# Block 0's last chunk by one level of Strassen's method, its second product beside the next block's first

## The chip, the core and the metric

The kernel runs on one core of one Trainium2 chip. The metric is the device time of one execution in microseconds (us); the time of a kernel is the median of its runs. Six parties matter here: TensorE (PE in the profile), which multiplies; VectorE (DVE), ScalarE (ACT) and GpSimd (POOL), which work elementwise; SyncE (SP), whose queue issues most transfers; and the DMA engines, which move data between HBM and the on-chip memory.

## The reference, cut to what matters

```python
kv  = np.einsum('bhsd,bhse->bhde', k, v)        # 8 batches, 8 heads, 576 rows, head size 64
out = np.einsum('bhsd,bhde->bhse', q, kv)
x   = out / sqrt(mean(out**2, -1) + 1e-6) * g_norm
x   = x.transpose(0, 2, 1, 3).reshape(4608, 512)  # rows x d_model
h   = x @ w_in                                  # w_in 512 x 2048
g   = np.maximum(0.01 * h, h)
return g @ w_out                                # w_out 2048 x 512
```

`w_in` and `w_out` arrive as float64. The kernel reads them as pairs of 32-bit words and rounds them to float32 on the chip.

## The kernel before, in words

**Tiling.** The 4608 rows of x are cut into 9 blocks of 512 rows (`NB`), and d_ff = 2048 into 4 chunks of 512 columns (`NC`; a chunk is 2 halves of 2 slices of 128, `U = 2`). For each block and chunk there are two products, both 512 x 512 x 512: h = W1 chunk times x block, and o = g chunk times W2 chunk, where o is summed over the chunks. x of a block is made by the attention part (`attention`, `outputs`, `divide`), whose steps are put between matmuls of the block before.

**How a chunk is multiplied.** Block 0 multiplies plainly (`first_block`, L1335). I call 2048 streamed columns a *unit*: for h, one slice of 128 d_ff columns, which is 4 matmuls of 128x512; for o, the same slice against 4 row groups, as 4 matmuls of 128x512 or 8 of 128x256. A plain chunk is 4 units for h and 4 for o. From block 1 on a chunk is multiplied by Strassen's method (`strassen`, L865): 7 products of 256 x 256 x 256 blocks, each 4 matmuls of 128x256, in the order `1, 2, 6, 5, 7, 3, 4`. Products 1, 6, 7 and 4 add up in one PSUM bank, 2, 5 and 3 in another, and after most of them ACT copies the bank or DVE adds it to SBUF before the next product may go on in that bank. Block 1 uses one level (`product_h`, `product_o`); later blocks use two levels for part of the work. The trace counts each float32 matmul as two records, so "x8" is 4 matmuls.

**What Strassen needs beside the products.** Sums of weight quarters for h (`sides_w1`, 4 additions of 128x512 a chunk, on GpSimd) and for o (`sides_w2`, 4, on GpSimd), sums of x quarters (`sides_x`, 4, on DVE, once a block), and sums of g quarters (`sums_of`, 4 a chunk, GpSimd, tiles `gs1` to `gs4`). `combine` makes the weight sums of the second level while block 1 runs: 8 additions on GpSimd (parts 0 and 1) and 8 on DVE (part 2) a chunk. They go to HBM for the later blocks.

**Rounding the weights.** The 32 weight tiles (`w_jobs`, here *jobs*) are loaded as raw 512 KB pieces into a ring of 7 places, 4 of them in `pairs`, which later holds Strassen's weight sums. A job is rounded by `round_f64` (L253): two ACT operations (`add`, `cut`; L271, L269), then on DVE a clamp (L273), a shift (L278), an or (L280) and an integer add (L285; two for a *halved* job). The temporaries live in the same `gs` tiles.

**Order.** Matmuls, rounding and most of SP's loads are held in program order (`pin`). In block 0 `between` (L1383) puts rounding jobs and attention steps after each half unit. The additions of `add` (L709) and the ACT operations on h and x were not held in order there; the builder's scheduler places them. In block 1 the second product of a chunk runs one chunk behind the first: `o_queue` holds `product_o`, and after `LAG = 2` slots one o product is issued beside each h product.

```python
        while half and rounded < min(3 * n + 8, 2 * n + 13, len(w_jobs) - (n < 11)):
            ...
            round_w(rounded)
            rounded += 1
```

After block 0's last unit its four accumulators are copied to `o_all` (L1371, L1373) and written out; then block 1 begins with chunk 0's h alone, because no o product is queued yet.

Of the kernel before, what the change touches and what calls it, by code (L numbers as in the profile page):

```python
# [11 lines left out]
U32 = mybir.dt.uint32  # L12
I64 = mybir.dt.int64
# [11 lines left out]
def kernel(  # L25
# [68 lines left out]
    steady = first_done = in_line = False  # L94

    def in_turn(ins):

        if steady or in_line:
            pin(ins)

# [126 lines left out]
    def spare(n, name, dtype=F32):  # L227
# [3 lines left out]
    raw_homes = itertools.cycle([view(stage, i * NW, NW) for i in range(3)]  # L231
                                + [pair(i, NW) for i in range(4)])
# [15 lines left out]
    def load_f64(src, eng):  # L248
        raw = next(raw_homes).bitcast(U32)
        load(split(raw, src), src, eng)  # L250
        return raw.rearrange("p (n two) -> p n two", two=2)
# [44 lines left out]
    w_jobs[1:-1] = [w_jobs[i + 1 if i % 2 else i - 1] for i in range(1, len(w_jobs) - 1)]  # L296
# [3 lines left out]
    def load_w(j, *eng):  # L300
        eng = eng or (nc.sync,)
        dst, src = w_jobs[j]
        if w_in.dtype == I64:
            w_raws[j] = load_f64(src.bitcast(U32), eng)
# [8 lines left out]
    def round_w(j):  # L313
        for _ in rounding(j):
            pass

# [73 lines left out]
    def outputs(b, lo, hi, e, sums, kv=None):  # L390


        x, n = x_of(lo, hi), hi - lo
        tiles = att_tiles("o_ps")
        o_ps = [t[:, :n] for t in tiles]
        o_products(b, lo, hi, e, o_ps)
        if kv is not None:
            kv_beside(b + 1, kv, tiles)
        for l in range(2):
            sq = t2k(n, "sq" if e else f"sum{l}")  # L400
            nc.scalar.activation(sq, o_ps[l], func=AF.Square)
            if e == 0:
                sums.append(sq)
            else:
                in_turn(nc.vector.tensor_add(sums[l], sums[l], sq))
        for l in range(2):
            nc.scalar.activation(x[:, 2 * l + e, :], o_ps[l], func=AF.Copy, scale=g_sb[:, e:e + 1])

    def divide(lo, hi, sums):
# [3 lines left out]
        for l in range(2):  # L413
# [4 lines left out]
            if l:  # L418
                act = nc.scalar.activation(rms, rms, func=AF.Sqrt, scale=1.0 / D, bias=eps_sb)
                if first_done:  # L420
                    pin(act)
# [3 lines left out]
        for l in range(2):  # L425
            t = t2k(n, "spread")
            nc.scalar.copy(t.rearrange("p (a i) -> p a i", i=E),
                           rms[:, l, :].unsqueeze(2).to_broadcast([P, n // E, E]))
            spread.append(t)
# [11 lines left out]
    def both_outputs(b, lo, hi, sums, kv=None, banks=None):  # L441
# [9 lines left out]
        for l in range(2):  # L451
            sq = t2k(2 * n, "sq").rearrange("p (e n) -> p e n", e=2)
            nc.scalar.activation(sq, o_ps[l], func=AF.Square)
# [9 lines left out]
        for l in range(2):  # L463
            for e in range(2):
                nc.scalar.activation(x[:, 2 * l + e, :], o_ps[l][:, e, :], func=AF.Copy,
                                     scale=g_sb[:, e:e + 1])
# [24 lines left out]
    def tail_of(b, lo, hi, fine=False, kv=(None, None), banks=None):  # L491
# [15 lines left out]
        for _ in divide(lo, hi, sums):  # L507
            if fine:
                yield
# [7 lines left out]
    def attention(b, apart=True, fine=False):  # L517
# [17 lines left out]
        for m in range(2):  # L535
# [9 lines left out]
            if not apart and m == 0:  # L545
                for p in (2, 3):
                    load_pair(b, p)
# [154 lines left out]
    later, tick = [], 0  # L702
# [5 lines left out]
    def add(eng, out_, a, b_, minus=False, pinned=False):  # L708
        ins = eng.tensor_tensor(out_, a, b_, op=ALU.subtract if minus else ALU.add)  # L709
        if pinned or steady:  # L710
            pin(ins)

    def sides_w1(c):
# [4 lines left out]
        s12 = pair(0, U, 2, 2, P)  # L718
        sides = {1: a11, 2: a12, 4: a22, 5: s12[:, :, :, 0, :], 6: s12[:, :, :, 1, :]}
        add(nc.gpsimd, sides[5], a21, a22)  # L720
        add(nc.gpsimd, sides[6], sides[5], a11, True)

        def more():
            s34 = pair(1, U, 2, 2, P)
            sides.update({7: s34[:, :, :, 0, :], 3: s34[:, :, :, 1, :]})
            add(nc.gpsimd, sides[7], a11, a21, True)
            add(nc.gpsimd, sides[3], a12, sides[6], True)
# [5 lines left out]
    writes = []  # L733

    def sides_w2(n):
# [7 lines left out]
        def sums(i):  # L743
            t = (t12, t34)[i]
            if n >= NC:
# [8 lines left out]
            if n == NC - 1:  # L754

                writes.append((w2_dram[c][i], t))
            else:
                pin(nc.sync.dma_start(w2_dram[c][i], t))
# [15 lines left out]
    def combine(c, part):  # L774
# [4 lines left out]
        parts = [((5, 6), pair(0, U, 2, 2, P))], [((7, 3), pair(1, U, 2, 2, P))], \  # L779
# [122 lines left out]
    def relu(t, src=None):  # L902
        with tc.issue_after(behind.pop()) if behind else nullcontext():
            nc.scalar.activation(t, t if src is None else src, func=AF.Prelu, alpha=SLOPE)  # L904
# [32 lines left out]
    def product_h(c, w_sides, x_sides, to):  # L937
# [3 lines left out]
        def done(i, bank):  # L941

            if i == 1:
                nc.scalar.copy(g11, bank)
            elif i == 5:
                nc.scalar.copy(g22, bank)
# [3 lines left out]
            elif i == 6:  # L950
                nc.scalar.copy(g21, bank)
# [9 lines left out]
        yield from strassen((("ha", "hc"), ("hb", "hd"))[c % 2], lambda i, part, r: w_sides[i][:, part, r, :],  # L961
                            lambda i, part, r: x_sides[i][:, r, :], done)
        yield from sums_of(c, to)

    more = consts.tile([P, 19, P], F32, name="more")
# [366 lines left out]
    def first_block(between):  # L1335

        accs = [ps_m.tile([P, DM], F32, tag=t, name="o_acc") for t in ("oa", "oc", "hb", "hd")]
        x, last = xTs.pop(0), None
        for n in range(2 * NC * U + 1):
            now = last  # L1340
            if n < 2 * NC * U:
                c, h, u = n // (2 * U), n // U % 2, n % U
                h_ps = ps_m.tile([P, NT], F32, tag=("ha", "hc")[n % 2], name="h_ps")

                parts = 2 if n == 0 else 1
                for part in range(parts):
                    cols = slice(part * NT // parts, (part + 1) * NT // parts)
                    for e in range(NE):
                        matmul(h_ps[:, cols], lhsT=w1_sb[h][c][:, u, e, :],
                               rhs=x[:, e, cols], start=(e == 0 and part == 0),  # L1350
                               stop=(e == NE - 1), skip_group_check=True)
                gT = view(g_all[n // 4 % 2], n % 4 * NT, NT)
                act = nc.scalar.activation(gT, h_ps, func=AF.Prelu, alpha=SLOPE)
                if n == 2 * NC * U - 1:
                    pin(act)
                last = (gT, w2_rows(h, c, u), n)
            if now is None:
                continue
            between(n, 0)
            for t in range(4):  # L1360
                halves = now[2] // U % 2
                for v in range(1 + halves):
                    cols = slice(v * N2, v * N2 + N2) if halves else slice(0, NT)
                    matmul(accs[t][:, cols], lhsT=now[0][:, t * P:(t + 1) * P],
                           rhs=now[1][:, v, :],
                           start=(now[2] == 0), stop=(n == 2 * NC * U), skip_group_check=True)
            between(n, 1)
        for t in range(4):
            o = o_homes[t].rearrange("p u n -> p (u n)")
            if t % 2:  # L1370
                nc.scalar.copy(o, accs[t])  # L1371
            else:
                nc.vector.tensor_copy(o, accs[t])  # L1373
            nc.scalar.dma_start(out[t * P:(t + 1) * P, :], o)

    first_attention()
    steps = {i: tail for tail in [tail_of(0, NT, S)] for i in (6, 8, 10)}
    a_steps = attention(1, False)
    steps.update((i, a_steps)
                 for i in (12, 13, 15, 16, 19, 20, 22, 23, 24))  # L1380
    loaded, rounded = 7, 5

    def between(n, half):  # L1383
        nonlocal loaded, rounded
        go(steps.get(2 * n + half, iter(())), 1)

        while half and rounded < min(3 * n + 8, 2 * n + 13, len(w_jobs) - (n < 11)):
            if loaded < len(w_jobs):
                load_w(loaded)
                loaded += 1  # L1390
                if loaded in (15, 19):
                    load_pair(1, (loaded - 15) // 4)
            round_w(rounded)
            rounded += 1
        if (n, half) == (12, 0):
            for p in range(2):
                load_pair(2, p)

    first_block(between)
    first_done = True  # L1400
    x_sides, _, sums, _ = sides_x(1)
    for _ in sums:
        pass
    for i, r in ((1, 0), (0, 1)):
        nc.gpsimd.tensor_copy(pair(i, U, 2, 2, P)[:1, 0, 0, r, :1], w2_1[:1, 1, NC - 1, U - 1, :1])
    h_sides, more_h = sides_w1(0)
    more_h()
    for part in range(2):
        sides_w2(0)[1](part)
    for part in range(2):  # L1410
        combine(0, part)
# [8 lines left out]

    SLOTS_3 = 10, 20, 22, 23
    WRITES_3 = 20, 21, 22, 23, 24, 25

    LAG = 2

    SPREAD = (2, 3, 9, 10, 12)
    o_queue, waited = collections.deque(), 0
# [8 lines left out]

    def go_o():
        while o_queue:
            if next(o_queue[0], o_queue) is not o_queue:
                return True  # L1440
            o_queue.popleft()

    for i in range(1, NB):
# [6 lines left out]
        for c in range(NC):  # L1450
# [7 lines left out]
            for t in range(7):  # L1458
                slot = 7 * c + t
                tick += 1  # L1460
                while later and later[0][0] <= tick:
                    later.pop(0)[1]()
# [39 lines left out]
                if slot == 4 and not one:  # L1502
                    while writes:
                        pin(nc.sync.dma_start(*writes.pop()))
                if one:
# [84 lines left out]
```

## Time and profile before

| | |
|---|---|
| median of 3 runs | 908.23 us (908.08 to 908.59) |
| the profiled execution, its own time | 908.56 us |
| its span, first to last instruction | 906.6 us |
| granted TensorE clock | 1.00 throughout |
| PE, busy share of the span | 99% |
| DVE, ACT, POOL | 67%, 37%, 58% |
| first unit of block 0 starts | 22.29 us |
| block 1's first product starts | 138.65 us |
| block 2's first product starts | 225.41 us |

The profiled execution took 908.56 us by its own time, of which 906.6 us lie between its first and its last instruction, so 1.96 us lie around the span. Every duration in this document is one record or one group of records of a profiled execution. In the views, "start us, us" are the start of a group and its length; the arrow shows the output tile, then the inputs; a bracket at the end says how long the engine sat idle before it and what ended that.

### The profile page before, as it was taken

Reading aid. Unit: us, or ns where it says so; the run is one execution under the profiler, and the core shown is the slowest. Engines: PE = TensorE matmul, PEld = TensorE weight load, DVE = VectorE, ACT = ScalarE, POOL = GpSimd, SP = SyncE. Lnnn points to the kernel's source line nnn. Section 1 sums busy time; section 2 is a strip of 40 time slices with the busy share of each in tenths; the row PEclk is TensorE's granted clock in tenths of the full one; section 3 lists DMA queues with packets and bytes.
Section 4 is the critical chain, followed back from the end, with each engine's and each line's share of the span. In section 5 each row is a group of like instructions: output and inputs, shape, how many; then the busy total and the mean of one; then the engine's idle time right before and its main releaser. Section 6 shows DMA issues by size and latency. Waiting matters only on the chain.

```text
span 906.6 us, 19091 instructions
## 1 busy us (share of the span) xinstructions
PE 899.4 (99%) x7344; PEld 789.7 (87%) x7344; DVE 610.8 (67%) x942; ACT 331.2 (37%) x645; POOL 525.0 (58%) x672
## 2 busy tenths in 40 slices
PE   8999999999999999999999999999999999999998
PEld 5555558888998999999999999999999999999997
DVE  5996856576674767685977498666877584646453
ACT  5663413231234332434333433343243424232420
POOL 2000255976738765766757584758477847883730
PEclk9999999999999999999999999999999999999999
DMA  9888436977799688968897798958886778677731
GB/s 322 260 260 266 151 98 195 306 251 244 253 306 329 204 279 256 307 219 261 252 322 263 218 298 255 321 170 271 250 284 188 230 207 277 203 234 226 258 111 59
DMA packets 109018, 219.00 MB, mean 242 GB/s; under 512 B 11264, under 2 KB 50560, under 8 KB 108928
## 3 DMA queue, kind: packets, MB, share of 16 engines
q1 hardware_dynamic: 105008, 212.22, 73.5%
q10 hardware_dynamic: 3472, 4.39, 1.4%
q8 instruction: 58, 0.95, 0.4%
q0 software_dynamic: 448, 1.18, 0.3%
q14 instruction: 32, 0.26, 0.1%
HBM read 187.34 MB, written 30.41 MB: 240 GB/s over the span
## 4 chain that ended last, share of the span: by engine, by line
PE 89%; DMA 4%; DVE 3%; POOL 2%; issue 1%; ACT 0%; SPq 0%; DVEq 0%; POOLq 0%; ACTq 0%
PE o_a L121 18%; PE o_c L121 14%; PE h_hd L121 9%; PE h_ha L121 9%; PE h_hc L121 9%; PE h_hb L121 8%; PE o_acc L121 6%; PE h_ps L121 6%; PE o_ps L121 3%; DMA q_in<-in_q_dram 2%; PE h_a L121 2%; PE h_b L121 2%; PE kv_ps L121 1%; PE h_d L121 1%; PE h_c L121 1%; DMA pairs<-in_v_dram 1%
## 5 line engine op out<-in xcount | busy, mean ns | idle before, releaser
L709 POOL TENSOR_TENSOR gs<-g 128x512 f32<-128x512 f32 x62 | 85.4, 1378 | 127.7 <-DVE w_all L709 60.3
L121 PE MATMUL o_a<-pairs,gs 128*128 128x256 f32 x472 | 111.9, 380 | 0.8 <-DMA pairs<-w 0.8
L709 DVE TENSOR_TENSOR o_all<-o_c,o_all 128x256 f32<-128x256 f32 (+2 forms) x124 | 69.4, 560 | 60.0 <-PE o_c L121 45.9
L904 ACT ACTIVATE g<-g 128x512 f32<-128x512 f32 x124 | 75.9, 631 | 62.4 <-DVE g L709 62.4
L709 DVE TENSOR_TENSOR g<-g,w_all 128x512 f32<-128x512 f32 (+1 forms) x84 | 87.9, 1046 | 15.2 <-POOL w_all L709 9.6
L709 POOL TENSOR_TENSOR w_all<-w_all 128x512 f32<-128x512 f32 x28 | 50.1, 1790 | 81.1 <-ACT w_all L1128 81.0
L121 PEld LDWEIGHTS o_a<-pairs,gs 128*128 128x128 f32 x472 | 85.5, 190 | 10.5 <-POOL more L709 1.0
L709 DVE TENSOR_TENSOR w_all<-h_ha,w_all 128x512 f32<-128x512 f32 x42 | 28.7, 684 | 55.0 <-PE h_ha L121 53.1
L1128 ACT COPY w_all<-h_hc 128x512 f32<-128x512 f32 x42 | 24.8, 590 | 105.9 <-PE h_hc L121 105.6
L1128 ACT COPY w_all<-h_ha 128x512 f32<-128x512 f32 x42 | 24.7, 587 | 104.5 <-PE h_ha L121 95.7
L121 PE MATMUL o_c<-pairs,gs 128*128 128x256 f32 x264 | 62.4, 379 | 0.0
L709 DVE TENSOR_TENSOR o_all<-o_a,o_all 128x512 f32<-128x512 f32 (+1 forms) x53 | 35.5, 669 | 37.5 <-PE o_a L121 36.8
L121 PE MATMUL o_a<-w,g 128*128 128x256 f32 x248 | 58.8, 379 | 0.0
L121 PE MATMUL h_ps<-xT,w_all 128*128 128x512 f32 (+1 forms) x136 | 58.1, 571 | 0.3 <-DVE w_all L285 0.3
L121 PE MATMUL o_acc<-w,g 128*128 128x256 f32 (+1 forms) x192 | 57.7, 451 | 0.0
L121 PEld LDWEIGHTS o_acc<-w,g 128*128 128x128 f32 x192 | 36.3, 190 | 21.5 <-issue 18.0
L709 DVE TENSOR_TENSOR g<-w_all 128x1024 f32<-128x1024 f32 x28 | 34.8, 1243 | 29.3 <-ACT w_all L1128 29.3
L709 POOL TENSOR_TENSOR pairs<-w 128x512 f32<-128x512 f32 x4 | 5.4, 1347 | 83.8 <-ACT cut L269 83.8
L121 PEld LDWEIGHTS o_c<-pairs,gs 128*128 128x128 f32 x264 | 47.9, 190 | 5.3
L121 PEld LDWEIGHTS o_a<-w,g 128*128 128x128 f32 x248 | 45.0, 190 | 4.9
L121 PEld LDWEIGHTS h_ps<-xT,w_all 128*128 128x128 f32 x136 | 25.4, 190 | 26.9 <-issue 24.9
L121 PE MATMUL h_hc<-stage,w_all 128*128 128x128 f32 x336 | 44.9, 276 | 0.0
(291 smaller groups left out, 2411.1 us busy)
## 6 DMA issues: line engine op xcount, KB each, us to landing
w_all<-w SPq DMA_DIRECT2D x196, 448.0 KB, 4.7
pairs<-w SPq DMA_DIRECT2D x94, 256.0 KB, 4.6
w<-w SPq DMA_DIRECT2D x22, 448.0 KB, 6.0
v_in<-in_v_dram SPq DMA_DIRECT2D x29, 288.0 KB, 5.6
k_in<-in_k_dram SPq DMA_DIRECT2D x28, 288.0 KB, 4.8
q_in<-in_q_dram SPq DMA_DIRECT2D x46, 144.0 KB, 4.8
q_in<-in_q_dram SPq DMA_DIRECT2D x46, 140.0 KB, 4.9
w<-stage SPq DMA_DIRECT2D x12, 512.0 KB, 3.6
```

The costliest lines, as they stand in the source:

```text
L121: pin(nc.tensor.matmul(*args, **kw))
L709: ins = eng.tensor_tensor(out_, a, b_, op=ALU.subtract if minus else ALU.add)
L904: nc.scalar.activation(t, t if src is None else src, func=AF.Prelu, alpha=SLOPE)
L1128: nc.scalar.copy(q[:, at], bank)
```

## The change

Block 0's chunks 0 to 2 stay plain. Its chunk 3 is multiplied by one level of Strassen's method. Its seven h products run beside the plain o units of chunk 2. Its seven o products (`product_o(-1, ...)`) are put into `o_queue` and run beside the first h products of block 1. What goes with that:

- Chunk 3's weight sums for h and block 0's x sums are made on DVE. Chunk 3's weight sums for o are made on GpSimd in block 0 and written to HBM, and block 1 reads them back instead of making them.
- `combine` of chunk 0 moves from before block 1 into block 1's slots 2, 3 and 6.
- The accumulators are copied to `o_all` by ACT alone, without writing out; the o products add to them, and the four parts of block 0's output are written from ACT's queue during block 1.
- The jobs are sorted so that chunk 0's four h weights come first, and block 0 starts with four h units in a row.
- From job 5 on a job's finishing steps are issued after the next job's first steps (`round_on`, `end_w`). Every second job from 6 on has its shift done by ACT (a Prelu with scale 2^60, written as int32) instead of DVE.
- In block 0 and at the change to block 1 the ACT operations and the additions are held in program order as well (`lined`, `in_first`), and the place of every step is written out by hand.

The core of the diff:

```diff
-    w_jobs[1:-1] = [w_jobs[i + 1 if i % 2 else i - 1] for i in range(1, len(w_jobs) - 1)]
+    w_jobs = [w_jobs[8 * c + 2 * i + second] for stage_ in
+              (((0, 0),), ((0, 1), (1, 0)), ((0, 2), (1, 1)), ((0, 3),), ((1, 2),), ((1, 3),))
+              for i in range(2 * U) for second, c in stage_]
...
+    half_way = collections.deque()
+    SIGNED = range(6, len(w_jobs), 2)
+
+    def end_w():
+        while half_way:
+            dst, add, cut, high, by_act = half_way.popleft()
...
+            if by_act:
+                pin(nc.scalar.activation(high.bitcast(I32), cut, func=AF.Prelu, scale=2.0 ** 60,
+                                         alpha=2.0 ** 127))
+            high, cut, dst = high.bitcast(U32), cut.bitcast(U32), dst.bitcast(U32)
+            if by_act:
+                pin(nc.vector.scalar_tensor_tensor(high, in0=cut, scalar=3, in1=high,
+                                                   op0=ALU.logical_shift_left, op1=ALU.bitwise_or))
+            else:
+                pin(nc.vector.tensor_scalar(high, cut, 3, None, op0=ALU.logical_shift_left))
+                pin(nc.vector.scalar_tensor_tensor(high, in0=cut, scalar=0x80000000, in1=high,
+                                                   op0=ALU.bitwise_and, op1=ALU.bitwise_or))
+            for at in range(2 if apart else 1):
+                i = slice(at, at + 1) if apart else slice(0, a)
+                pin(nc.vector.tensor_tensor(dst[:, i], high[:, i], add[:, i], op=ALU.add))
+
+    def round_on(j):
...
+        pin(nc.scalar.activation(add, raw[:, :, 0], func=AF.Copy, scale=2.0 ** -29))
+        pin(nc.scalar.activation(cut, raw[:, :, 1].bitcast(F32), func=AF.Copy, scale=2.0 ** -112))
+        pin(nc.vector.tensor_scalar(cut, cut, HIGH_MOST, -HIGH_MOST, op0=ALU.min, op1=ALU.max))
+        end_w()
+        half_way.append((dst, add, cut, high, j in SIGNED))
...
-            if n >= NC:
+            if n >= NC - 1:
                 pin(nc.sync.dma_start(t, w2_dram[c][i]))
                 return
...
+    ROUND_0 = 5, 6, 8, 9
+    ROUND_1 = 11, 12, 14, 15, 17, 18, 19, 20, 21, 22, 24, 25, 26, 27, 28, 29
+    ROUND_3 = 30, 31, 32
+    TAIL_1 = 2, 3, 4
+    A_1 = 5, 6, 8, 9, 10, 11, 12, 13, 14
+    A_3 = 0, 1, 3, 4, 5, 5, 6
+    X_1, S_1 = 12, 14
+    UNITS = 2, 2, 2, 3, 2, 3, 2
...
+        for n in range(2 * U):
+            relu_h = plain_h(0, n)
+            round_to(ROUND_0[n])
+            relu_h()
...
+        for c in range(1, NC - 1):
+            o_steps = plain_o(c - 1)
+            for n in range(2 * U):
+                for half in range(2):
+                    at = 4 * U * (c - 1) + 2 * n + half
+                    if half:
+                        go(o_steps, 4)
+                    else:
+                        relu_h = plain_h(c, n)
+                    round_to(ROUND_1[at])
+                    if not half:
+                        relu_h()
...
+        o_steps = plain_o(NC - 2)
+        g_sides = {}
+        h_steps = product_h(-1, w_sides, x_sides, g_sides)
+        for t in range(7):
+            later_steps()
+            if t < len(ROUND_3):
+                round_to(ROUND_3[t])
+            go(h_steps, 1)
+            if t == 0:
+                for x_add in x_adds[2:]:
+                    add(nc.vector, *x_add)
+                more_h()
+            go(o_steps, UNITS[t])
+            go(a_steps, A_3.count(t))
...
+            elif t == 3:
+                pin(nc.gpsimd.tensor_copy(more_all[:1, :1], w2_1[:1, 1, NC - 1, U - 1, :1]))
+                next_sides, more_h = sides_w1(0)
+            elif t == 5:
+                for i in range(2):
+                    sides_w2(-1)[1](i)
+                next_x, _, sums, _ = sides_x(1)
+                go(sums, 2)
...
+        for copy, to, part in take:
+            pin(copy(to, part))
+        o_queue.append(product_o(-1, g_sides, os, store(0)))
...
-                    if t == 1:
+                    if t == (1 if c else 3):
                         combine(c, 2)
+                    if slot in LATE_0:
+                        combine(0, LATE_0.index(slot))
```

The order in which the built program of the changed kernel stands on each engine can be read without running it, and the prediction refers to it as *the built order*: which instruction follows which on an engine, and which instruction each waits for.

More of the change, by code (lines that the diff above doesn't have):

```diff
@@ L12 @@
 U32 = mybir.dt.uint32
+I32 = mybir.dt.int32
 I64 = mybir.dt.int64
@@ L229, in spare @@
         return gpool.tile([P, n], dtype, tag=next(spare_homes), name=name)
-    raw_homes = itertools.cycle([view(stage, i * NW, NW) for i in range(3)]
-                                + [pair(i, NW) for i in range(4)])
+    raw_homes = [view(stage, i * NW, NW) for i in range(3)] + [pair(i, NW) for i in range(4)]
     def split(t, src):
@@ L246, in load, with load_f64 @@
             pin(eng[i * len(eng) // len(t)].dma_start(to, part))
-    def load_f64(src, eng):
-        raw = next(raw_homes).bitcast(U32)
+    LAST = 32
+    last_spare = itertools.cycle([pair(i, 2, NT)[:, h] for i in range(2) for h in range(2)])
+    def load_f64(j, src, eng):
+        raw = raw_homes[j % 7 if j < LAST else (j - LAST) % 3].bitcast(U32)
         load(split(raw, src), src, eng)
@@ L507, in tail_of @@
         for _ in divide(lo, hi, sums):
-            if fine:
+            if fine or b == 1 and in_first:
                 yield
@@ L699, in first_attention @@
             round_w(j)
-    later, tick = [], 0
+    more_all = consts.tile([P, 19 * P], F32, name="more")
+    more = view(more_all, 0, 19, P)
+    later, tick = [], -7
     def put_off(n, what):
@@ L943, in done @@
             if i == 1:
-                nc.scalar.copy(g11, bank)
+                lined(nc.scalar.copy(g11, bank))
             elif i == 5:
-                nc.scalar.copy(g22, bank)
+                lined(nc.scalar.copy(g22, bank))
             elif i == 2:
@@ L950, in done @@
             elif i == 6:
-                nc.scalar.copy(g21, bank)
+                lined(nc.scalar.copy(g21, bank))
             elif i == 3:
@@ L1333, in store @@
         return finish
[L1335 to L1380, printed above, removed]
+    o_queue, waited = collections.deque(), 0
+    LAG = 2
+    def go_o():
+        while o_queue:
+            if next(o_queue[0], o_queue) is not o_queue:
+                return True
+            o_queue.popleft()
     loaded, rounded = 7, 5
-    def between(n, half):
+    PAIR_AT = {12: 0, 14: 1}
@@ L1384, in between, with round_to @@
+    def round_to(n):
         nonlocal loaded, rounded
-        go(steps.get(2 * n + half, iter(())), 1)
-        while half and rounded < min(3 * n + 8, 2 * n + 13, len(w_jobs) - (n < 11)):
+        while rounded < n:
             if loaded < len(w_jobs):
@@ L1390, in between @@
                 loaded += 1
-                if loaded in (15, 19):
-                    load_pair(1, (loaded - 15) // 4)
-            round_w(rounded)
+                if loaded in PAIR_AT:
+                    load_pair(1, PAIR_AT[loaded])
+            round_on(rounded)
             rounded += 1
[L1395 to L1411, printed above, removed]
+        if n == len(w_jobs):
+            end_w()
+    def later_steps():
+        nonlocal tick
+        tick += 1
+        while later and later[0][0] <= tick:
+            later.pop(0)[1]()
+    ROUND_0 = 5, 6, 8, 9
@@ L1459 @@
                 slot = 7 * c + t
-                tick += 1
-                while later and later[0][0] <= tick:
-                    later.pop(0)[1]()
+                later_steps()
                 go(a_steps, 0 if one else fine[1].get(slot, 0))
```

152 lines of the change are left out of this document (112 added, 40 removed).

## The prediction

> **What bounds the kernel now.** I read the page first: its busy shares and the row of slices.
>
> ```profile
> PE 899.4 (99%) x7344; PEld 789.7 (87%) x7344; DVE 610.8 (67%) x942; ACT 331.2 (37%) x645; POOL 525.0 (58%) x672
> ...
> PE   8999999999999999999999999999999999999998
> ```
>
> TensorE is idle for 906.6 - 899.4 = 7.2 us of the span. The view of waits, for PE over the first 260 us, says where it waits at all:
>
> ```profile
> PE idle_ps L121 <- DVE group L323: 1.5, 1, 1.5
> PE kv_ps L121 <- DMA pairs<-in_v_dram: 0.5, 1, 0.5
> PE sum_ps L644 <- ACT flat L639: 0.4, 1, 0.4
> PE h_ps L121 <- DVE w_all L285: 0.3, 1, 0.3
> ```
>
> All four lie before 26.4 us. The last matmuls end at 903.1 us (the timeline's last group, 902.49 + 0.61), 3.5 us before the span does. So 2.7 us of the idle time lie at the start, 3.5 at the end, and 1 us in all the rest: no later wait stands ready to take up what block 0 saves. Time saved or lost on PE in block 0 is saved or lost in the end.
>
> PE's timeline gives the prices. I read start to start, since the ends of pipelined matmuls overlap:
>
> ```profile
> 22.29 3.72 PE L121 MATMUL h_ps<-xT,w_all 128*128 128x256 f32 x16
> 26.34 3.70 PE L121 MATMUL h_ps<-xT,w_all 128*128 128x512 f32 x8 [0.33 <-DVE w_all L285]
> ...
> 128.31 3.60 PE L121 MATMUL h_ps<-xT,w_all 128*128 128x512 f32 x8
> 131.74 7.07 PE L121 MATMUL o_acc<-w,g 128*128 128x256 f32 x32
> 138.65 1.89 PE L121 MATMUL h_a<-xT,w_all 128*128 128x256 f32 x8
> ...
> 152.94 1.89 PE L121 MATMUL h_b<-xT,w_all 128*128 128x256 f32 x8
> 154.66 1.89 PE L121 MATMUL h_d<-xT,w_all 128*128 128x256 f32 x8
> 156.39 1.89 PE L121 MATMUL h_b<-xt,pairs 128*128 128x256 f32 x8
> ```
>
> A plain h unit takes 131.74 - 128.31 = 3.43 us, a plain o unit (138.65 - 131.74) / 2 = 3.455, a Strassen product 1.72 to 1.73.
>
> **The sum on PE.** Removed: chunk 3's 4 h and 4 o units, 4 x 3.43 + 4 x 3.455 = 27.5 us. Added: 14 products x 1.725 = 24.15. That is 3.4 us less. The built order agrees: 24 matmuls of 128x512 and 16 of 128x256 go, 56 of 128x256 come, 2048 columns or one unit less; all others remain. The attention's matmuls between them are as many as before.
>
> What can take this back is a new wait. I place PE's work in the built order by these prices. After 26.34 come 19 units (65.4) and four pieces of attention (0.5, 1.3, 1.3 and 1.0, from how much longer the steps between units are where they hold one, 40.18 to 103.02): Strassen's h begins at 96 us. Seven products (12.1), chunk 2's four o units (13.8) and a fifth piece (1.0) later, at 123, block 1 begins. Check: 138.65 - 13.8 for chunk 3's o, which now comes later, - 1.7 for its h = 123.15. "Due" below is when PE would reach the matmul that needs a thing.
>
> **Rounding, block 0.** The loads only change order; jobs 0 to 4 are rounded by the same instructions, so the 0.33 us wait stays. Job 4 is done on DVE at 33.0. A plain job costs DVE 2.25 us (clamps at 23.95 and 26.20); a job whose shift goes to ACT saves 0.46, so 1.8, on average 2.03. The later finishing lets a clamp come in between: job 5 is done at 35.7, job 10 at about 45.8, job 19, with some 5 us of attention work on DVE, at about 69. They are due at 40.1 (o unit 1), 57.9 and 92.7: margins 4.4, 12 and 24 us, which is the cover. Without it a late job costs its lateness. ACT gets 13 operations more, 0.57 to 0.7 us each, 9 us at most, at 37% busy; no row has a Prelu into int32, so I take the ACT rows of this size, 0.57 (start to start) to 0.7; a gain is excluded, as it is added work. New waits: a relu of h now stands behind ACT's shift, which waits for DVE's clamp, and behind it the next job's two operations. The lag is about one job (2.25 us); the relu's PSUM bank is due two units (6.9 us) later. Hidden. On SP the loads of jobs 23 and later stand behind key loads of block 1's attention, whose buffers PE frees with the first kv piece at 62.6; job 23 would land near 70, and ACT reaches it at about 74, after the relu of the unit that ends at 69.6. Hidden; if not, its lateness moves chunk 3's h sums, which are due at 104.
>
> **Additions.** Chunk 3's h sums and block 0's x sums (8 on DVE, 0.69 to 1.2 us, 5.5 to 9.6 in all) mostly fill DVE's gap (before, it idled 6.3 us at 82 to 89). The four g sums on GpSimd (1.27 to 1.79 each, 5.1 to 7.2) and `combine` of chunk 0 (8 additions, 120 to 128 us before) come into block 1; seven additions to `o_all` (0.69) replace copies on DVE. Accumulator copies on ACT (4 x 0.59, due only when the o product begins at 129), the output writes (4 issues on ACT, 0.35 to 0.5) and the read-back of `t12`, `t34` (two 512 KB transfers; this kernel's land in 4 to 6.7 us, due 13.8 us or more after release) have covers of several us. In the built order an output write on ACT also waits until an earlier transfer has landed: the fourth until about 154, and behind it stands the copy that block 1's chunk 1 needs at 158.7; the cover is 4 us.
>
> **The change to block 1.** Here margins are thin. I add rows along the built order:
> - h product 5 needs DVE's addition of product 2. The attention's piece ends on PE at 100.6; ACT works on it for 1.9 (107.69 to 109.59), until 102.6, then on job 30 (1.15); DVE does the clamp, job 29's last steps and the addition (0.46 + 1.8 + 0.69): 106.7, due 107.6. Margin 0.9.
> - GpSimd may start when ACT has read job 31, at 108.5. From then on DVE has eight operations on jobs 30 and 31, 3.75 us by themselves (104.38 to 106.33 for a job's last four), done at 112.3; then the attention's last reductions 1.3, product 7's addition (due 119.7), product 3's at 117.8 and block 1's x: 0.64 + 2.06 + 0.63 + 2.15 = 5.5, at 123.3, due 124.8. Margin 1.5.
> - `combine` part 2 of chunk 0 (2.5 us at 142.98) stands on DVE ahead of a transpose of q (1.25) and of the addition that frees the bank for block 1's product 4. It starts after the addition of the first waiting o products (the second ends on PE at 134.3), at 135.2; with 2.5, 1.25 and 0.69 it is done at 139.6, due 142.6. Margin 3.
> - GpSimd must do 14 additions of 512 and 5 of 256 to reach the g sum of the first waiting o product: 14 x 1.27 + 5 x 0.72 + 0.3 = 21.7, at 130.2, due 137.4. Margin 7.2.
>
> DVE and GpSimd do not run freely side by side:
>
> ```profile
> 91.94 1.55 DVE L285 CUSTOM_DVE_ANT_0 w_all<-w_all,add 128x1024 uint16<-128x1024 uint16 x1
> 93.42 1.48 DVE L273 TENSOR_SCALAR cut<-cut 128x512 f32<-128x512 f32 x1
> ...
> 97.50 0.68 DVE L285 CUSTOM_DVE_ANT_0 w<-w,add 128x1024 uint16<-128x1024 uint16 x1
> ```
>
> ```profile
> 91.67 1.27 POOL L709 TENSOR_TENSOR pairs<-w,pairs 128x512 f32<-128x512 f32 x1
> 92.90 1.71 POOL L709 TENSOR_TENSOR pairs<-w,w 128x512 f32<-128x512 f32 x1
> ```
>
> The integer add takes 1.55 us beside GpSimd and 0.68 alone, the clamp 1.48 against 0.42. Before, GpSimd was idle from 128.2 to 146.6, and only x was made beside it; now it is busy from 108.5 on. If half the operations are caught, the eight take 7.4 instead of 3.75 and x comes at 124.4; `combine` takes 5 and its addition comes at 142.2: both 0.4 us early. So the waits lie between 0 and the 5.6 us of the slower rival. I take 0.5, near the free end, as half caught still costs nothing while margins of 0.4 to 0.9 will not all hold.
>
> The Trainium skill ("SBUF — State Buffer", section "Who interferes with whom") says that a DVE instruction with two SBUF inputs, or in a two-port mode, and a GpSimd instruction that reads SBUF exclude each other for the whole instruction. These rows agree. By that rule with every operation caught, the sum would be the slower rival's.
>
> **Sum.** 908.56 - 3.4 + 0.5 = 905.7 us of the profiled execution, which lies 0.33 above the median; for the median 905.4.
>
> **Rivals.**
> *Every DVE operation is caught* (slower, 9%). The eight operations take 11 us (rows of 1.28 to 1.55): 119.5, the addition for product 4 at 121.5, 1.8 late; x then ends at 128.4, another 1.8 late; `combine` takes 7.7 (157.72 to 165.39, where GpSimd ran), and its addition comes 2.0 late. 5.6 in all: 910.4. For it: three eligible operations in a row were caught at 91.9 to 96.3. Against: at 112.9 to 114.3 four were not, as GpSimd paused, and each catch also delays GpSimd. It is slower than before once the waits exceed 3.4 us.
> *GpSimd's chain is late* (slower, 3%). At 2.12 us (its longest row here) per addition of 512 and 1.35 per 256, 36.7 us: 145.2, 7.8 late: 912.6. The mean of 1.79 gives 2.4 late. Against: most rows are 1.27.
> *Part is caught* (same, 14%): waits of 1.6 to 5.2 us, 906.4 to 910.
> *A wait of the fixed order that I priced as hidden* (same, 4%): a relu or load 2 to 3 us late, 907 to 908. Against: no PE wait in 40 to 140 us before.
> *Nothing is saved*: the two forms could cost the same per unit. The rows exclude it.
>
> **How the numbers follow.** The measurement can tell about 0.2%, 1.8 us. Waits of 0 to 1.6 us (70%) are faster, 904.8 to 906.4; partial catches and hidden waits 18%; the two slower rivals 12%. The range goes from 904.6 (every margin holds, with 0.2 of spread) to 909.0, which leaves out the slower rivals and the upper end of the partial one.
>
> **What would show it.** PE's timeline after: block 1's h_a near 123 us, block 2's first h_ha near 222 instead of 225.41. Each wait over 0.3 us on h_a or h_c between 107 and 145 refutes a margin; waits on h_ps or o_acc before 96 refute the rounding; DVE rows of 1.3 to 1.5 us after 108.5 show the catches. Wrong altogether if block 2 starts after 225.4.

## The result, and the profile after

| | before | after |
|---|---|---|
| median | 908.43 us (6 runs, 908.08 to 909.05) | 905.45 us (6 runs, 905.27 to 906.20) |
| the profiled execution, its own time / span | 908.56 / 906.6 us | 905.58 / 903.9 us |
| first unit of block 0, block 1, block 2 start | 22.29, 138.65, 225.41 us | 22.75, 123.69, 223.80 us |
| last group of matmuls starts | 902.49 us | 899.84 us |

The ratio after to before is 0.9968, with a 95% interval of 0.9957 to 0.9978: 3.0 us less. The forecast was 905.4.

The page of the changed kernel: PE is as full as it was.

```profile
PE 896.3 (99%) x7376; PEld 795.9 (88%) x7376; DVE 619.8 (69%) x945; ACT 340.7 (38%) x663; POOL 529.1 (59%) x675
```

The span is 903.9 us, so PE is idle for 7.6 us of it (before, 7.2). The view of waits for PE (what waited, for what; us in total, times, the longest) names one that is new:

```profile
PE h_a L128 <- DVE g L766: 1.0, 1, 1.0
```

Before the change no Strassen product waited for DVE. PE's timeline (start, length, group; in brackets the idle time ahead of it and what ended it) shows where:

```profile
123.69 1.89 PE L128 MATMUL h_a<-xT,w_all 128*128 128x256 f32 x8
...
141.43 1.89 PE L128 MATMUL o_a<-pairs,gs 128*128 128x256 f32 x8
144.31 1.99 PE L128 MATMUL h_a<-g,w_all 128*128 128x256 f32 x8 [0.99 <-DVE g L766]
146.14 1.89 PE L128 MATMUL o_c<-pairs,gs 128*128 128x256 f32 x8
```

The wait stands ahead of block 1's product 4, the place of the third margin of the prediction. A group follows the one before it after 1.725 us; here it took 2.88 and the next one 1.83, so the 0.99 us of idle time cost 1.26 us. DVE's timeline says why product 7's addition, which frees the bank `h_a`, came late:

```profile
135.65 0.76 DVE L766 TENSOR_TENSOR stage<-w_all 128x256 f32<-128x256 f32 x1
...
141.01 1.35 DVE L766 TENSOR_TENSOR stage<-w_all 128x128 f32<-128x128 f32 x1
142.29 0.28 DVE L766 TENSOR_TENSOR stage<-w_all,stage 128x128 f32<-128x128 f32 x1
142.49 1.25 DVE L579 STREAM_TRANSPOSE qT<-q_in 128x576 f32<-128x576 f32 x1
143.59 0.67 DVE L766 TENSOR_TENSOR g<-h_a,g 128x512 f32<-128x512 f32 x1
```

The rows `stage<-` are the eight additions of `combine` part 2 of chunk 0. They take 6.9 us (135.65 to 142.57). Before the change the same eight took 2.5 us, and GpSimd stood idle for 18.42 us around them (DVE's first and last of the eight, and GpSimd's next row, in the kernel before):

```profile
142.98 0.42 DVE L709 TENSOR_TENSOR stage<-w_all 128x256 f32<-128x256 f32 x1
...
145.25 0.28 DVE L709 TENSOR_TENSOR stage<-w_all,stage 128x128 f32<-128x128 f32 x1
```

```profile
146.59 1.28 POOL L709 TENSOR_TENSOR pairs<-w_all 128x512 f32<-128x512 f32 x1 [18.42 <-PE h_c L121]
```

In the changed kernel the last one took 0.28, the one ahead of it, of the same size, 1.35. GpSimd worked beside all but the last, which fell into its pause from 142.22 to 142.62:

```profile
137.50 1.77 POOL L766 TENSOR_TENSOR stage<-pairs 128x256 f32<-128x256 f32 x2
...
140.90 1.32 POOL L766 TENSOR_TENSOR gs<-g,gs 128x512 f32<-128x512 f32 x1
```

### The profile page after: what moved, and what is told of

Same layout as the page of the kernel before. It is cut to its first block, busy times and chain, and to the rows that moved or that the text cites. A ratio compares the mean times of both kernels' runs of the same rounds, so it can differ in the third digit from the quotient of the medians.

```text
span 903.9 us, 19186 instructions
## 1 busy us (share of the span) xinstructions
PE 896.3 (99%) x7376; PEld 795.9 (88%) x7376; DVE 619.8 (69%) x945; ACT 340.7 (38%) x663; POOL 529.1 (59%) x675
## 4 chain that ended last, share of the span: by engine, by line
PE 93%; POOL 2%; DVE 2%; DMA 1%; issue 1%; ACT 0%; DVEq 0%; POOLq 0%; ACTq 0%
PE o_a L128 20%; PE o_c L128 16%; PE h_hd L128 10%; PE h_ha L128 9%; PE h_hc L128 9%; PE h_hb L128 9%; PE o_acc L128 5%; PE h_ps L128 4%; PE o_ps L128 3%; PE h_a L128 2%; PE h_c L128 2%; PE h_b L128 2%; PE h_d L128 1%; PE kv_ps L128 1%; DMA pairs<-in_v_dram 1%; POOL more L766 1%
## 5 line engine op out<-in xcount | busy, mean ns | idle before, releaser
L766 POOL TENSOR_TENSOR gs<-g 128x512 f32<-128x512 f32 x64 | 88.0, 1376 | 128.2 <-DVE w_all L766 60.9
L766 DVE TENSOR_TENSOR o_all<-o_c,o_all 128x256 f32<-128x256 f32 (+1 forms) x128 | 72.1, 564 | 62.3 <-PE o_c L128 47.0
L766 POOL TENSOR_TENSOR pairs<-w_all 128x512 f32<-128x512 f32 x6 | 8.0, 1330 | 109.3 <-ACT cut L366 101.6
L128 PE MATMUL o_c<-pairs,gs 128*128 128x256 f32 x280 | 66.2, 379 | 0.0
L766 DVE TENSOR_TENSOR o_all<-o_a,o_all 128x512 f32<-128x512 f32 (+1 forms) x56 | 37.5, 670 | 39.4 <-PE o_a L128 38.8
L128 PEld LDWEIGHTS o_c<-pairs,gs 128*128 128x128 f32 x280 | 51.0, 190 | 5.7
L766 POOL TENSOR_TENSOR gs<-gs,g 128x512 f32<-128x512 f32 x32 | 43.7, 1367 | 2.2
L128 PEld LDWEIGHTS h_ha<-stage,w_all 128*128 128x128 f32 x336 | 43.1, 192 | 1.8 <-issue 0.3
L128 PE MATMUL h_ha<-stage,w_all 128*128 128x128 f32 x336 | 44.4, 275 | 0.0
L128 PE MATMUL o_acc<-w,g 128*128 128x256 f32 (+1 forms) x144 | 44.2, 453 | 0.0
```

Source lines behind the costliest of these rows:

```text
L128: pin(nc.tensor.matmul(*args, **kw))
```

## Where the 3 us come from

I measure each trace from its own first unit, as the start-up differs from run to run (22.29 to 23.03 us). The last three rows are the experiments that settle the sum; they are told below.

| kernel | first unit to block 1 | first unit to block 2 | block 2 to last group | median |
|---|---|---|---|---|
| before (two profiles) | 116.36, 116.35 | 203.12, 203.12 | 677.08, 676.88 | 908.43 |
| after (two profiles) | 100.94, 100.94 | 201.05, 200.96 | 676.04, 676.02 | 905.45, 905.34 |
| the new order, chunk 3 plain (`e3_plain`) | 116.36 | 203.12 | 676.05 | 908.24 |
| after, four GpSimd additions left out (`e2_quiet`) | 100.93 | 199.78 | 676.37 | 904.54 |
| after, GpSimd held back (`e4_behind`) | 100.93 | 199.78 | 676.02 | 904.31 |

Between the two profiled executions, 908.56 and 905.58 us, the 2.98 us are: 203.12 - 199.78 = 3.34 us saved on PE; 201.05 - 199.78 = 1.27 us given back by the one wait; 1.04 us saved behind block 2's start; 0.46 us lost in the start-up; 0.05 us at the end of the span and 0.28 us outside it (1.96 us before, 1.68 after; spans are given to 0.1 us, so only the 0.33 of the two together is firm). -3.34 + 1.27 - 1.04 + 0.46 - 0.05 - 0.28 = -2.98.

The 1.04 us are one wait in the kernel before, far from the change, for the read of a weight sum from HBM. It stands in both of its profiles (PE's timeline, first and second profile):

```profile
576.58 1.97 PE L121 MATMUL o_a<-pairs,gs 128*128 128x256 f32 x8 [0.82 <-DMA pairs<-w]
```

```profile
576.67 1.97 PE L121 MATMUL o_a<-pairs,gs 128*128 128x256 f32 x8 [0.63 <-DMA pairs<-w]
```

It is in no profile of the changed kernel or of a variant, though `e1_late` has one of the same kind elsewhere (0.91 us at 283.39, for a load of v). In the plain variant SP issues the loads of these sums 1.2 to 1.9 us earlier (568.28 and 571.52 us, against 570.17 and 573.36 in the first profile and 569.57 and 572.76 in the second), yet that kernel's median is within 0.2 us of the one before, and the kernel before also has runs of 907.7 us. So it need not happen in each run, and whether the change makes it rarer stays open. PE's own gain up to block 2 is 3.34 - 1.27 = 2.1 us and about 0.3 us lies outside the span. That makes 2.4 of the 3.0 us between the medians; on the chip of the second profile of the changed kernel the medians differ by 3.2 us (908.53 and 905.34) and the fastest runs by 2.6 (907.78 and 905.15). What is left, some 0.2 to 0.8 us, can be this wait in some of the runs; it is not shown.

## The experiments

**The kernel before and the changed kernel again.**

> The kernel before, profiled a second time. In its first profile PE waited 0.82 us at 576.58 us for the read of a weight sum from HBM (o_a, DMA pairs<-w), far from the change; in the changed kernel's profile it did not. If such a wait comes by chance, it is missing here or stands in another place, and the span is about 905.6 instead of 906.6 us (the wait took 1.05 us of PE's time from start to start). If it belongs to the order of the transfers in the kernel before, it is here again at the same place, and the changed kernel owes about 1 us of its gain to having lost it.

Measured: 908.65 us, span 906.7, the wait at the same place, 0.63 us. This is one run, and it speaks for the second account without settling it (see above).

> The changed kernel again, beside the next three on one chip. In its first profile PE waited once after block 0, 0.99 us ahead of block 1's product 4. If that wait belongs to the order, it is here again within 0.1 us, and the median is 905.2 to 905.7.

Measured: 905.34 us (905.15 to 905.44); the wait ahead of product 4 is 0.90 us. It belongs to the order, not to one run.

**Is it Strassen's method or the new order?** The loop over chunk 3 becomes plain, in the changed kernel's order of jobs, rounding and steps:

```diff
-        h_steps = product_h(-1, w_sides, x_sides, g_sides)
-        for t in range(7):
+        for t in range(8):
...
-            go(h_steps, 1)
...
-            go(o_steps, UNITS[t])
+            if t % 2:
+                go(o_steps, 4)
+            else:
+                plain_h(NC - 1, t // 2)()
...
-        o_queue.append(product_o(-1, g_sides, os, store(0)))
+        for part in range(3):
+            combine(0, part)
+        go(plain_o(NC - 1))
```

> The changed kernel's order of jobs, late finishing, shift on ACT and fixed order, but chunk 3 multiplied plainly in block 0, as before (16 units, seven o products fewer in block 1, no x sums and no g sums for it; combine of chunk 0 ahead of block 1 again). My account: all of the gain is the 27.5 - 24.15 us of PE; without it the time is that of the kernel before, within 0.5 us: 907.9 to 908.9 (the wait of product 4 cannot occur). Block 1 starts near 138.7 us. Rival, the new order and rounding bring the gain: 905 to 906.5 us. Other rival, they cost something that Strassen's method had to pay for: 909.5 or more.

Measured: 908.24 us, ratio to before 0.9998 (0.9989 to 1.0007), and PE's times up to block 2 are those of before to 0.01 us. Together the order, the late finishing and the shift on ACT neither gain nor cost anything there: all that PE gains up to block 2 comes from the products.

**Each half alone.** First h by Strassen's method and o plain, on the plain variant:

> The plain variant (e3_plain) with chunk 3's h alone by Strassen's method: seven products beside chunk 2's plain o, with the x sums and h weight sums that they need on DVE; chunk 3's o stays plain, 4 units behind them, in block 0. My account: the sum on PE is made of two parts that add up, and this one is worth 4 x 3.43 - 7 x 1.725 = 1.65 us: 908.24 - 1.65 = 906.6 us, up to 0.3 more if the first plain o unit waits for the last relu. Rival, the h part costs waits of its own (its bank hand-overs have margins of 0.9 and 1.5 us): 907.2 or more, with waits on h_a or h_c between 97 and 125 us.

Measured: 910.03 us (1.0019 of before, 1.0010 to 1.0028), slower than either kernel, so the expectation failed by 3.4 us, and the waits came behind 125 us, not where its rival looked for them. Block 1 began 114.71 us after the first unit, 1.65 us earlier than in the plain variant, as the sum says; then product 6 waited 2.02 us and a later product 0.52. ACT's timeline (ACTq rows are issues of transfers), and PE's:

```profile
140.15 0.37 ACTq L1540 DMA_DIRECT2D out_dram<-o_all  x1
140.56 0.58 ACT L1538 COPY o_all<-o_acc 128x512 f32<-128x512 f32 x1 [4.83 <-DMA w<-w_all]
...
143.08 0.59 ACT L1003 COPY g<-h_a 128x512 f32<-128x512 f32 x1
```

```profile
143.77 1.97 PE L128 MATMUL h_a<-xt,more 128*128 128x256 f32 x8 [2.02 <-POOL stage L766]
```

I had put block 0's output writes on ACT's queue between its copies. ACT stood 4.83 us at a write, by the view until an earlier transfer had landed, and the copy that frees `h_a` came behind the writes, at 143.08. The releaser that the view names, GpSimd, is not what held PE: product 6 was waiting for that copy. The next kernel moves the writes to SP's queue, slots 1 to 4 of block 1:

```diff
-            nc.scalar.dma_start(out[i * P:(i + 1) * P, :], o)
+            put_off(2 + i, functools.partial(lambda i, o: pin(nc.sync.dma_start(out[i * P:(i + 1) * P, :], o)), i, o))
```

> The h part alone once more, with block 0's output writes on SP's queue in block 1's slots 1 to 4 instead of on ACT's queue between its copies. In the first trial PE reached block 1 exactly 1.65 us earlier than the plain variant (114.71 against 116.36 us behind the first unit), but then waited 2.02 us ahead of product 6, because ACT's copy of product 1 stood behind three output writes that waited for earlier transfers, and 0.52 us later. My account: that wait belongs to where the writes stood, not to Strassen's method; without it 908.24 - 1.65 = 906.6 us, up to 907.0 by the writes among SP's loads. Rival, the h part by itself costs what it saves: 908 us or more again, with a wait on h_a or h_c in block 1.

Measured: 906.93 us (0.9988 of before, 0.9979 to 0.9997). The 2 us wait is gone; 0.29 us is left at 155.48 (h_b, for ACT's copy). It is for such a wait that the prediction gave the output writes a cover of 4 us. In the changed kernel they stand in another place and the cover held: the fourth goes out at 155.70 us, and the copy behind it still waits for PE until 156.71. The other half, on `e4_behind` below, with g written in quarters by two ACT operations a unit:

```diff
...
-            go(h_steps, 1)
...
+                plain_h(NC - 1, t // 2, True)()
...
-        go(h_steps)
+        go(sums_of(-1, g_sides))
```

> The other half, in the order of e4_behind: chunk 3's h plain (four units, g written in quarters by two ACT operations a unit), its o by Strassen's method beside block 1's first h. My account: against e4_behind it gives back the 1.65 us of the h part, 904.31 + 1.65 = 905.95 us, and against the plain variant it gains 4 x 3.455 - 7 x 1.725 = 1.75 us and whatever the plain variant loses by chance: 905.9 to 906.5. Rival, what the o products bring into block 1 costs as much as they save: 907 us or more, with waits on h_a, h_c or o_c between 125 and 150 us.

Measured: 906.47 us (0.9979 of before, 0.9971 to 0.9988). Block 2 starts 201.44 us after the first unit, 1.68 us earlier than in the plain variant and 1.66 later than with both halves. So, without the waits, h brings 1.65 and o 1.68, together 3.33 of the 3.34 measured with both.

**What holds up product 4?** Two kernels move DVE's additions, and one takes their neighbour away.

```diff
-                    if t == (1 if c else 3):
+                    if t == (1 if c else 4):
                         combine(c, 2)
```

> The changed kernel with combine part 2 of chunk 0 issued one slot later, behind the addition of product 7. My account: the eight additions on DVE were what held that addition until 144.3 us; with them out of its way it is done near 138.6, product 4 starts when PE reaches it, and the wait (1.16 us from start to start, and 0.1 us in the step after it) is gone: 904.2 us. The additions then end near 147.3, and the addition of the o product before the next one in that bank comes at about 148.6, due 148.3: up to 0.3 us of a new wait, so 904.2 to 904.5. Rival, the hand-over only moves: DVE is late by as much at the next hand-over, and the time stays at 905.4.

Measured: 907.06 us (905.56 to 909.68). The wait of product 4 is gone, and others are there. GpSimd's timeline, and PE's:

```profile
112.13 1.66 POOL L766 TENSOR_TENSOR stage<-pairs 128x256 f32<-128x256 f32 x2
```

```profile
128.97 1.96 PE L128 MATMUL h_a<-xt,more 128*128 128x256 f32 x8 [0.86 <-DVE xt L766]
```

With another rotation of its buffers the scheduler let GpSimd make four additions of chunk 1 from 112 us on. DVE's eight operations on jobs 30 and 31 then took 8.7 us, from 108.82 to 117.47 (6.8 in the changed kernel; the 8.1 of the next expectation leaves out the first clamp), and x, the second margin of the prediction, was late: 0.23 and 0.86 us of idle time. That is the slower rival's mechanism, in part. Two more waits stand further on: 0.59 us at 191.62 (`o_c`, for DVE) and the 0.91 us for v. The expectation failed because the edit changed more than it meant to. With the buffers kept as they were:

```diff
...
+                    if slot == 3:
+                        kept = iter([next(stage_homes), next(stage_homes)])
+                    if slot == 4:
+                        combine(0, 2, kept)
```

> DVE's combine of chunk 0 behind product 7's addition again, but in the same places of its ring of buffers as in the changed kernel, so that GpSimd does up to 138.8 us what it does there (in the first trial of this order it made four additions of chunk 1 as early as 112 us). My account: DVE's eight operations on jobs 30 and 31 take 6.8 us again, not 8.1, x is in time, and neither product 4 nor the products before it wait: 904.2 to 904.9 (the end of that range if the o product that uses the same bank as the one before 148 us comes up to 0.7 us late). Rival: the later combine itself is what cost the 1.6 us of the first trial, through the loads and writes queued behind it and the later additions on DVE: 906 to 907.1.

Measured: 905.26 us (904.49 to 906.43), between the two accounts; the eight operations take 6.8 us, x is in time, product 4 does not wait. But there is a wait that `e1_late` had too:

```profile
190.63 1.97 PE L128 MATMUL o_c<-pairs,gs 128*128 128x256 f32 x8 [0.60 <-DVE o_all L766]
```

Behind the later `combine` GpSimd's own sums run later, so that they now meet DVE's `combine` of chunk 3: four of its eight additions take 1.35 to 1.49 us; in the changed kernel two were long (1.23 and 1.46). Moving the work on DVE moved the collision, and 0.84 us of the 1.27 came back; neither account had this.

The next kernel leaves out four of GpSimd's additions, so what it computes is not the product; it serves only for the comparison.

```diff
+            if (c, part) == (1, 0):
+                t = y.rearrange("p u r j m -> p (u r) j m")
+            else:
                 add(eng, s1, y21, y22, pinned=part == 2)
...
```

> The changed kernel with DVE's order untouched, but with the four additions on GpSimd that ran from 137.5 to 140.9 us left out (the second-level sums of chunk 1's first part are not formed; raw quarters are written in their place). If what stretched DVE's eight additions from 2.5 to 6.9 us was GpSimd beside them, those that lose the neighbour fall to 0.28 to 0.4 us, the eight take 3 to 4.5 us, product 7's addition is done by 142 and the wait of product 4 is gone: 904.2 us. Rival, the additions are long for another reason (their place in memory, the transfers beside them): rows of 0.76 to 1.4 us stay, the wait stays, 905.4 us.

Measured: 904.54 us (904.15 to 905.35), no wait of product 4. DVE's timeline:

```profile
137.62 1.48 DVE L766 TENSOR_TENSOR stage<-w_all 128x256 f32<-128x256 f32 x1
139.03 0.41 DVE L766 TENSOR_TENSOR stage<-w_all,stage 128x256 f32<-128x256 f32 x1
139.36 0.28 DVE L766 TENSOR_TENSOR stage<-w_all 128x128 f32<-128x128 f32 x1
...
141.38 0.68 DVE L766 TENSOR_TENSOR g<-h_a,g 128x512 f32<-128x512 f32 x1
```

DVE's order is that of the changed kernel. GpSimd's last addition ends at 138.8 us; DVE's rows fall from 1.48 to 0.41 and 0.28 from then on, the eight take 4.8 us instead of 6.9, and product 4 starts when PE reaches it, at 143.06. The neighbour is the cause.

**A version that keeps all the work.** GpSimd's `combine` of chunk 1 is issued behind the second part of chunk 0's, which reuses a buffer that DVE's additions must first have left:

```diff
-                    if slot in LATE_0:
-                        combine(0, LATE_0.index(slot))
+                    if slot == 2:
+                        combine(0, 0)
+                    if slot == 6:
+                        next(stage_homes)
+                        for at in ((0, 1), (1, 0), (1, 1)):
+                            combine(*at, True)
...
```

> The changed kernel with nothing left out, DVE's order as it was, and GpSimd's combine of chunk 1 (both parts) held behind the second part of chunk 0's, which waits for DVE's own additions to be written out. So GpSimd stands idle from about 138.8 us until DVE is through, and its twelve additions come behind it. My account: as with the additions left out, DVE's eight take 4.8 us, product 7's addition is done at 142, product 4 starts without a wait: 904.3 to 904.6 us, a valid kernel faster than the changed one by 0.9. Rival, GpSimd's later work is late for the o sums of chunk 0 (due near 162 us; I put them at 160): a new wait of 1 us or more, 905.3 or above.

Measured: 904.31 us (903.92 to 904.84), against 905.34 (905.15 to 905.44) for the changed kernel on the same chip; ratio to before 0.9954 (0.9942 to 0.9967). GpSimd's timeline, and DVE's first and last of the eight:

```profile
142.08 0.73 POOL L766 TENSOR_TENSOR stage<-more 128x256 f32<-128x256 f32 x1 [4.14 <-DVE g L766]
```

```profile
136.39 0.42 DVE L766 TENSOR_TENSOR stage<-w_all 128x256 f32<-128x256 f32 x1
...
139.53 0.28 DVE L766 TENSOR_TENSOR stage<-w_all,stage 128x128 f32<-128x128 f32 x1
```

GpSimd idles 4.14 us, DVE's eight take 3.4 us, and no product of block 1 waits. GpSimd's later sums are ready in time, so the rival with its 1 us falls.

**Rounding.** `SIGNED = ()` leaves every shift to DVE.

> The changed kernel with every job's shift on DVE (13 operations of 0.42 us there, 13 of 0.62 us fewer on ACT). My account: rounding has a cover of 4 to 24 us until job 29, so nothing there reaches PE; only job 30's shift stands in the thin place, 0.42 us (0.9 if GpSimd holds it up) against margins of 0.9 and 1.5: 905.2 to 905.9. Rival: DVE's load in block 0 counts, the jobs come late: each us of lateness costs one, 906.5 or more, with waits on h_ps or o_acc before 96 us.

Measured: 905.66 us (905.38 to 907.11); no wait on h_ps or o_acc after 26.4 us. The only new idle time is product 4's, 1.21 instead of 0.90 to 0.99 us. The rounding is hidden, as expected; the shift on ACT by itself brings nothing that this comparison can separate.

## Why the prediction was right, point by point

**The sum on PE**: predicted -3.4, measured -3.34 and, by halves, -1.65 and -1.68. Placed in before's clock (0.46 us less), Strassen's h began at 96.26 (predicted 96) and block 1 at 123.23 (123). Block 2 came at 223.34 instead of 222: 201.05 - 199.78 = 1.27 is the wait.

**Rounding**: job 5 was done at 35.5 (predicted 35.7); no wait between 26.4 and 141 us. ACT's shift took 0.61 to 0.67 us, inside the bounds.

**The margins**, in before's clock: product 2's addition was done at 106.8 (106.7), due 107.7: held. The eight operations took 6.8 us (7.4 by half caught), x was done at 123.4 (123.3 to 124.4): held. `combine` started at 135.2 (135.2) but took 6.9 us where I had put 5.0, and its addition was done at 143.8 (142.2), due 142.7: lost. GpSimd reached the first waiting o product's g sum at 135.7 (130.2), due 137.5: held, with 1.8 us left of 7.2.

**The step that was mis-sized** is the waits: taken at 0.5, measured 1.27. I chose a value near the free end because "half caught" still left 0.4 us for `combine`. But seven of its eight additions were longer than alone, as GpSimd had its own chain running without a pause just then. The same mistake sits in GpSimd's chain: I priced it at its free rows (1.27 us), while its three rows of 512 between 122.9 and 128.4 took 1.73 to 2.13, and it stood 2.29 us until job 31 was rounded. (Of the 14 additions of 512 in that sum, one had already run at 80.4 us.) The 6.9 us lie between the prediction's half-caught 5 and the 7.7 of the slower rival.

**What hid that**: two terms that I had at zero. The transfer wait of the kernel before (1.04 us) was part of its own time, on which I built the sum, and I took it to stay; and 0.28 us went outside the span. Against them stood 0.46 us of start-up. So 905.4 rests on 3.34 us that were forecast to 2%, and on luck: errors of 0.77 us (the wait) and -0.91 us (these terms) that cancelled to 0.14.

**The rivals**: the slower one did not happen in the changed kernel, but `e1_late` shows its mechanism, and `e7_h_only` came out 3.4 us above its forecast, as much as the whole change saves on PE, with the output writes ahead of a copy on ACT's queue. A rotation of buffers or the place of a write made the difference.

## What to carry to other kernels

On an engine that is 99% busy the columns that a change takes away were worth their price to 2% here, and what has to be found out is which hand-over becomes late. Price two-input additions that run on DVE while GpSimd adds nearer to the rows where every one is caught than to a mean (6.9 us here, against 7.7 and 5), and look for the hand-overs whose margin is smaller than that. If one is lost, hold GpSimd back until DVE is through (by a buffer that it must wait for) rather than move DVE's work, which here met GpSimd again further on.

## What the runs showed of the hardware

**Who is caught.** DVE's additions with both inputs in SBUF stretched beside GpSimd from 0.28 to 1.35 us (128x128) and from 0.41 to 1.48 (128x256). The addition `g<-h_a,g`, which has one input in PSUM, took 0.67 us at 143.59 while GpSimd was adding, and 0.68 when it was idle; the transpose took 1.25 us either way. The Trainium skill ("SBUF — State Buffer", section "Who interferes with whom") says that a DVE instruction with at most one SBUF input, outside the two-port modes, does not contend with GpSimd. These rows agree. So in a collision only part of DVE's queue gets longer. The operands tell most of it, but not all: the clamp has one SBUF input and was caught as well in the prediction's rows (1.48 us against 0.42).

**What a gap on PE costs.** The idle time in brackets is less than what the gap takes from start to start: 0.99 us cost 1.27, 1.21 (`e6_shift`) cost 201.26 - 199.78 = 1.48, 0.60 (`e5_order`) cost 200.62 - 199.78 = 0.84, and the 0.82 us of the kernel before cost 1.04. About a quarter of a us comes on top of each. The rows show how it is made up: a group's 1.89 us reach 0.16 past the start of the next one, 1.725 later, and the group behind a gap is 0.08 to 0.10 longer (1.97 to 1.99).

**Outside the span.** The own time exceeds the span by 1.94 to 2.06 us in the runs of the kernel before, by 1.88 to 1.98 in the plain variant and by 1.68 to 2.03 in the two kernels with h alone, but by 1.66 to 1.82 in all runs of kernels where block 0's last o runs in block 1. What causes it stays open.
